# Replicating gate values over partitions through a DRAM scratch instead of 64 shifted copies

## The chip, the cores and the metric

The kernel runs on one core of one Trainium2 chip. The metric is the device time of one execution in microseconds. The profile's span, from the first to the last instruction, is about 1.9 us shorter than that time. Most executions of one kernel lie within a few tenths of a microsecond, so a difference of 0.5 us (0.2%) is about the smallest that five rounds can show. In the views, PE stands for the matmuls of TensorE and PEld for its weight loads, ACT for ScalarE, DVE for VectorE, POOL for GpSimd, SPq for the queue in which SyncE issues DMAs; a PSUM bank is a piece of the memory that matmuls write to.

## The reference

The output is a mix of two branches over 2048 tokens of width 512, with a gate g per token:

```python
g = _sigmoid((x * gate_w).sum(-1, keepdims=True))
a = _A_ref(x, A_wq, A_wk, A_wv, A_wo, A_beta)     # 4 segments of 512 tokens, 32 heads of 16
b = _B_ref(x, B_W_gate, B_W_up, B_W_down)         # gated FFN, 512 -> 1792 -> 512
return g * a + (1 - g) * b
# in _A_ref, per segment s and head:
#   p = softmax(q k^T * scale + causal mask);  a_dot = p v
#   o = sigmoid(beta) * (phi(q) M / (phi(q) z + 1e-6)) + (1 - sigmoid(beta)) * a_dot
#   M, z are then updated with phi(k), v of this segment
```

The change touches only small things: where exp of the gate logit lies in memory, and constants made from beta.

## The kernel before

The kernel builds a list of operations with estimated durations. A list scheduler (`Sched`), whose tie-breaks depend on a seed, then fixes one static order for each engine. So any change of an operation or of the seed can move every instruction. The gate part and the constants:

```python
sc = Sched(seed=59)
...
cst = [act(... V.eb = exp(V.braw) ...)]
cst.append(dve(... V.romgh = V.eb + 1 ...))
cst.append(dve(... V.epsv = V.romgh * EPS ...))
for s2 in range(2):
    for tt in range(4):        # the column of ones, scaled, beside V in vaug
        cst.append(dve(lambda e, s2=s2, tt=tt: e.tensor_copy(V.vaug[:, s2, tt, :, 16], V.romgh[:, :]), 190, ...))
...
for c in range(NSEG):
    # c == 0: POOL multiplies x by gate_w (gml), ACT sums each product (gad); gate_w comes by DMA into gwb
    # c > 0: x is loaded again, DVE multiplies and sums (gate)
    gq["act"].append(act(... gx = exp(V.gl[:, t0:t1]) ..., name="gexp"))
    ...
    for a in range(4):
        for jj in range(4):    # 16 copies a segment, 32 partitions x 4 values each
            dst = V.gexpT[32 * jj:32 * jj + 32, 16 * c + 4 * a:16 * c + 4 * a + 4]
            gq["flex"].append(... dve or act: copy dst <- V.gexp[32 * a:32 * a + 32, t0:t1] ...)
```

The one reader of gexpT is `rdg` on DVE, which scales the attention output of each head group. TensorE runs three kinds of work. Ordinary matmuls use the whole array (projections and FFN, 512 columns). Score quads are four or eight matmuls on 32 rows each (x4 or x8 in the views); each quad writes four PSUM banks that one large exp on ACT (2048 columns) must read before the next quad may write them. PV groups use four column tiles. For the order of the start it matters that ACT has one queue:

```python
acts.append(act(lambda a, e=e: a.activation(V.E[:, e, :, :], PL[:, :, :], ACT.Exp, scale=SCALE), t_act(2048),
                reads=[f"bankL{b}" for b in range(4)], writes=[f"E{e}"], name=f"exp{s}_{tag}"))
```

The softmax here doesn't subtract the row's maximum and nothing guards it: scores larger than these inputs give would overflow.

Of the kernel before, what the change touches and what calls it, by code (L numbers as in the profile page):

```python
# [8 lines left out]
ACT = mybir.ActivationFunctionType  # L9
# [3 lines left out]
F32 = mybir.dt.float32  # L13
# [11 lines left out]
def t_act(n, psum=True, ap=0):  # L25
    return (174.0 if psum else 198.0) + 0.834 * n + 93.0 * ap


def t_dve(n, rate=1):
    return 155.0 + n / rate / 0.96  # L30
# [336 lines left out]
def plan(S, D, F):  # L367
    NT, KT, NF = S // 128, D // 128, F // 128
    return [
        ("xT", [128, KT, S], BF16), ("wq", [128, KT, 512], BF16), ("wk", [128, KT, 512], BF16), ("wv", [128, KT, 512], BF16),  # L370
        ("wo", [128, 4, 512], BF16), ("wg", [128, KT, F], BF16), ("wu", [128, KT, F], BF16), ("wd", [128, NF, 512], BF16),
        ("qT", [128, 8, 512], BF16), ("kT", [128, 4, 512], BF16), ("kp", [128, 12, 512], BF16),
        ("phiq", [128, 4, 512], BF16), ("ek", [128, 4, 512], BF16), ("phik", [128, 4, 512], BF16), ("ttmp", [128, 2, 512], BF16),
        ("vaug", [128, 2, 4, 32, 17], BF16), ("E", [128, 8, 4, 512], BF16),
        ("Tn", [128, 2, 512], F32), ("adT", [128, 512], BF16), ("oTt", [128, 512], BF16),
        ("amem", [128, 2, 512], BF16), ("amemT", [128, 4, 512], BF16), ("oT", [128, 8, 512], BF16),
        ("hT", [128, 20, 512], BF16), ("rl", [128, 3, 512], BF16), ("osb", [128, 3, 512], BF16),
        ("Mbd", [128, 4, 136], F32), ("Mbd16", [128, 4, 136], BF16), ("mumask", [128, 2, 136], BF16), ("mutmp", [128, 2, 136], F32),
        ("braw", [128, 32], BF16), ("eb", [128, 32], F32), ("romgh", [128, 32], F32), ("epsv", [128, 32], F32),
        ("gexp", [128, NT], F32), ("omg", [128, NT], F32), ("gexpT", [128, NT * 4], F32), ("c2g", [128, 2, 4, 32], F32), ("gwb", [128, 512], BF16), ("gl", [128, NT], F32),  # L380
        ("rden", [128, 32], F32), ("rdg", [128, 32], F32), ("rdm", [128, 128], F32), ("pm8", [128, 8], F32), ("pm", [128, 2], F32), ("ident", [128, 128], BF16),
    ]


def build_kernel(nc, A_x, A_wq, A_wk, A_wv, A_wo, A_beta, W_g, W_u, W_d, gate_w, out):
    _, S, D = A_x.shape
    F = W_g.shape[1]
    assert D == 512 and S % 512 == 0 and F % 128 == 0
    NSEG, KT, NF, NT = S // 512, D // 128, F // 128, S // 128
    EPS, SCALE = 1e-6, 16 ** -0.5  # L390
    sc = Sched(seed=59)
    T = {}
    with contextlib.ExitStack() as stack:
        for name, shape, dt in plan(S, D, F):
            T[name] = stack.enter_context(nc.sbuf_tensor(name, shape, dt))
        PL = stack.enter_context(nc.psum_tensor("psL", [128, 4, 512], F32))
        PA = [stack.enter_context(nc.psum_tensor(f"psA{i}", [128, 512], F32)) for i in range(4)]
        for st in sc.streams:
            sc.sem[st] = stack.enter_context(nc.semaphore(f"s_{st}"))
        program(sc, nc, T, PL, PA, A_x, A_wq, A_wk, A_wv, A_wo, A_beta, W_g, W_u, W_d, gate_w, out, NSEG, KT, NF, NT, EPS, SCALE)  # L400
        with nc.Block() as block:
            sc.emit(block)
    return sc


def program(sc, nc, T, PL, PA, A_x, A_wq, A_wk, A_wv, A_wo, A_beta, W_g, W_u, W_d, gate_w, out, NSEG, KT, NF, NT, EPS, SCALE):
    V = type("V", (), T)

    def op(eng, fn, occ, **k):
        return sc.add(Op([(eng, fn, occ)], **k))  # L410
# [7 lines left out]
    def dve(fn, occ, **k):  # L418
        return op("dve", fn, occ, **k)

    def act(fn, occ, **k):
        return op("act", fn, occ, **k)

    def pool(fn, occ, **k):
        return op("pool", fn, occ, **k)

    def dma(eng, fn, nbytes, occ=500.0, **k):
        return op(eng, fn, occ, dma=True, nbytes=nbytes, **k)
# [81 lines left out]
    for i in range(4):  # L510
# [5 lines left out]
        dst = V.xT[:, :, i * 128:(i + 1) * 128]  # L516
# [10 lines left out]
    cst = [act(lambda e: e.activation(V.eb[:], V.braw[:], ACT.Exp), 300, reads=["braw"], writes=["eb"], name="eb")]  # L527
    cst.append(dve(lambda e: e.tensor_scalar(V.romgh[:], V.eb[:], 1.0, None, ALU.add), 190, reads=["eb"], writes=["romgh"], name="romgh"))
    cst.append(dve(lambda e: e.tensor_scalar(V.epsv[:], V.romgh[:], EPS, None, ALU.mult), 190, reads=["romgh"], writes=["epsv"], name="epsv"))
    for s2 in range(2):  # L530
        for tt in range(4):
            cst.append(dve(lambda e, s2=s2, tt=tt: e.tensor_copy(V.vaug[:, s2, tt, :, 16], V.romgh[:, :]), 190, reads=["romgh"], writes=[f"vone{s2}_{tt}"], name="vone"))
    sc.queue(0, [t for t in cst if t.eng == "act"])
    sc.queue(1, [t for t in cst if t.eng == "dve"])

    gexpT_r = {}
    gq = {"pe": [], "act": [], "dve": [], "flex": [], "pool": [], "sp": []}
    for c in range(NSEG):
        t0, t1 = 4 * c, 4 * c + 4
        gx = V.gexp[:, t0:t1]  # L540
        if c == 0:
            for t in range(4):
                gq["pool"].append(pool(lambda e, t=t: e.tensor_tensor(V.Tn[:, t % 2, :], V.hT[:, t, :], V.gwb[:], ALU.mult), 1250, reads=[f"hT{t}", "gwb"], writes=[f"Tn{t % 2}"], name=f"gml{t}"))  # L543
                gq["act"].append(act(lambda e, t=t: e.activation(V.Tn[:, t % 2, :], V.Tn[:, t % 2, :], ACT.Copy, accum_out=V.gl[:, t:t + 1]), t_act(512, False) + 100, reads=[f"Tn{t % 2}"], writes=[f"Tn{t % 2}", f"gl{t}"], name=f"gad{t}"))
        else:
            for t in range(t0, t1):
                ld = dma("sp", lambda e, t=t: e.dma_start(V.osb[:, 2, :], A_x[0, t * 128:(t + 1) * 128, :]), 1 << 17, writes=["osb2_0", "osb2_1"], name=f"ldxr{t}")
                ld.after = GATE_T[c] + 4000.0 * (t - t0)
                gq["sp"].append(ld)
                gq["dve"].append(dve(lambda e, t=t: e.tensor_tensor_reduce(out=V.osb[:, 2, :], in0=V.osb[:, 2, :], in1=V.gwb[:], scale=1.0, scalar=0.0, op0=ALU.mult, op1=ALU.add, accum_out=V.gl[:, t:t + 1]),  # L550
                                     t_dve(512) + 70, reads=["osb2_0", "osb2_1", "gwb"], writes=["osb2_0", "osb2_1", f"gl{t}"], name=f"gate{t}"))
        gq["act"].append(act(lambda e, t0=t0, t1=t1, gx=gx: e.activation(gx, V.gl[:, t0:t1], ACT.Exp), 215, reads=[f"gl{t}" for t in range(t0, t1)], writes=[f"gexp{c}"], name="gexp"))
        om = V.omg[:, t0:t1]
        gq["dve"].append(dve(lambda e, om=om, gx=gx: e.tensor_scalar(om, gx, 1.0, None, ALU.add), 180, reads=[f"gexp{c}"], writes=[f"omg1{c}"], name="omg1"))
        gq["dve"].append(dve(lambda e, om=om: e.reciprocal(om, om), 250, reads=[f"omg1{c}"], writes=[f"omg{c}"], name="omg"))
        gexpT_r[c] = []
        for a in range(4):
            for jj in range(4):
                dst = V.gexpT[32 * jj:32 * jj + 32, 16 * c + 4 * a:16 * c + 4 * a + 4]
                gq["flex"].append(sc.add(Op([("dve", lambda e, a=a, dst=dst, t0=t0, t1=t1: e.tensor_copy(dst, V.gexp[32 * a:32 * a + 32, t0:t1]), 200),  # L560
                                             ("act", lambda e, a=a, dst=dst, t0=t0, t1=t1: e.activation(dst, V.gexp[32 * a:32 * a + 32, t0:t1], ACT.Copy), 215)],
                                            reads=[f"gexp{c}"], writes=[f"gexpT{c}_{a}{jj}"], name="gexpT")))
                gexpT_r[c].append(f"gexpT{c}_{a}{jj}")

    def c2g(s):
        t0 = 4 * s
# [2 lines left out]
    sc.queue(1, gq["act"])  # L569
    sc.queue(1, gq["pool"])  # L570
    sc.queue(1, gq["dve"])
    sc.queue(2, gq["flex"])
    sc.queue(3, gq["sp"])

    def kslot(s, n):
# [53 lines left out]
        return pes, evs, sbs, acts, sps  # L629

    def va(s):
        return [f"va{s % 2}_{tt}" for tt in range(4)] + [f"vone{s % 2}_{tt}" for tt in range(4)]

    def mu(s):
        pes, ds, ps = [], [], []
# [206 lines left out]
    a, b, c_, d, e_ = proj(0)  # L842
    put(pproj=a, dproj=b, dsb=c_, aphi=d, spk=e_)
    slots = None
    for s in range(NSEG):
# [6 lines left out]
        a, b, c_, d, e_ = att(s, between)  # L852
        put(patt=a, exp=b, pool=c_, datt=d, ppv=e_)
        if s < NSEG - 1:
            a, b, c_ = mu(s)
            put(pmu=a, dmu=b, poolmu=c_)
            a, b, c_, d, e_ = proj(s + 1)
            put(pproj=a, dproj=b, dsb=c_, aphi=d, spk=e_)
        a, b, slots = ffn(s)
        put(pffn=a, effn=b)  # L860
    a, b, c_ = outp(NSEG - 1, slots)
# [39 lines left out]
def bass_gated_mix__memory_aug_infini_attn__glu_gated_reglu__prompt_kernel(  # L901
    nc, A_x, A_wq, A_wk, A_wv, A_wo, A_beta, B_x, B_W_gate, B_W_up, B_W_down, gate_w, out
):
    return build_kernel(nc, A_x, A_wq, A_wk, A_wv, A_wo, A_beta, B_W_gate, B_W_up, B_W_down, gate_w, out)
# [28 lines left out]
```

## Time and profile before

273.07 us median of 3 runs (272.86 to 273.07).

| | before |
|---|---|
| span | 271.2 us |
| PE / DVE / ACT / POOL busy | 97 / 76 / 75 / 37% |
| chain that ended last, on PE | 88% |

The page's line of busy times (us, share of the span, instructions) and its shares of the chain, kernel before:

```profile
PE 263.0 (97%) x2108; PEld 115.1 (42%) x2143; DVE 204.8 (76%) x382; ACT 203.7 (75%) x210; POOL 99.5 (37%) x156
...
PE 88%; ACT 2%; DVE 2%; DMA 2%; issue 2%; POOL 2%; ACTq 1%; DVEq 0%; POOLq 0%
```

What the change takes away, from the groups by form of the kernel before (line, engine, operation, tiles, shapes, count | busy us, mean ns | idle before it):

```profile
L561 ACT ACTIVATE gexpT<-gexp 32x4 f32<-32x4 f32 x57 | 11.6, 203 | 1.4
...
L560 DVE COPY gexpT<-gexp 32x4 f32<-32x4 f32 x7 | 2.4, 344 | 0.2
L532 DVE CAST vaug<-romgh 128x32 bf16<-128x32 f32 x8 | 1.9, 349 | 0.0
```

A busy PE is modelled, so the question whether TensorE ever waits is better asked of its weight loads. The timeline of weight loads of the kernel before, at the start (start us, duration us, what, count, [idle before <- releaser]):

```profile
11.98 0.96 PEld L602 LDWEIGHTS psA<-xT,wk 128*128 128x128 bf16 x5
13.94 0.10 PEld L698 LDWEIGHTS psL<-qT,kp 32*128 32x128 bf16 x4 [1.00 <-DVE kp L616]
14.27 2.70 PEld L600 LDWEIGHTS psA<-wv,xT 128*128 128x128 bf16 x14 [0.23 <-issue]
17.80 0.12 PEld L698 LDWEIGHTS psL<-qT,kp 32*128 32x128 bf16 x8 [0.83 <-ACT E L703]
18.13 0.11 PEld L600 LDWEIGHTS psA<-wv,xT 128*128 128x128 bf16 x2 [0.21 <-issue]
```

(kp is the masked copy of the keys that a quad needs, made on DVE.) Ordinary loads follow one another every 0.216 us. Between the last ordinary load and a quad the least that occurs is 0.522 us, a switch of 0.306 us more. Anything longer is a stall. A load takes 0.10 us, so the last of the five wk loads starts at 11.98 + 0.96 - 0.10 = 12.84; the first quad comes at 13.94, that is 1.10 later, a stall of about 0.57 us. For the second quad, the last load ahead starts at 14.27 + 2.70 - 0.10 = 16.87, and 17.80 is 0.93 later, a stall of 0.41. These two, 0.98 us in all, are the only stalls of note in the whole span. The same two are in the view of PE's waits (us in total, times, longest; counted from the modelled end of the matmul before, so a little less):

```profile
PE psL L698 <- DVE kp L616: 0.5, 1, 0.5
PE psL L698 <- ACT E L703: 0.3, 1, 0.3
```

The second comes from ACT's queue. Its timeline, kernel before: the gate exp, four of the copies to be removed, and an exp for the keys stand before the first attention exp (E), which the second quad needs:

```profile
13.78 0.20 ACT L552 ACTIVATE gexp<-gl 128x4 f32<-128x4 f32 x1
14.01 0.89 ACT L561 ACTIVATE gexpT<-gexp 32x4 f32<-32x4 f32 x4
14.93 1.06 ACT L584 ACTIVATE ek<-kT 128x1024 bf16<-128x1024 bf16 x1
15.89 1.86 ACT L703 ACTIVATE E<-psL 128x2048 bf16<-128x2048 f32 x1
```

### The profile page before, as it was taken

What the parts mean: (1) busy time and instruction counts of PE and PEld (TensorE: products, weight loads), DVE (VectorE), ACT (ScalarE), POOL (GpSimd) and SP (SyncE); (2) the same over time, 40 slices, a digit from 0 to 9 for tenths busy, and PEclk for the clock granted to TensorE, in tenths of its full rate; (3) what the DMA queues carried; (4) which work ended last, traced back from release to release, by engine and by line L of the source; (5) the groups of instructions that cost most, each with busy time, mean ns of one, the idle gap of its engine ahead of it and who ended that gap; (6) DMA issues with size and microseconds to landing.
All of it is one profiled execution on the core that took longest, in us unless ns stands there. A gap on an engine that the chain in (4) does not pass through costs nothing.

```text
span 271.2 us, 5268 instructions
## 1 busy us (share of the span) xinstructions
PE 263.0 (97%) x2108; PEld 115.1 (42%) x2143; DVE 204.8 (76%) x382; ACT 203.7 (75%) x210; POOL 99.5 (37%) x156
## 2 busy tenths in 40 slices
PE   8989999999999999999999999999999999999996
PEld 4433343444444444444343444343434444344444
DVE  4689988899889799999888887877773547776300
ACT  3499998898989987899768779887776768682122
POOL 5614343454533253643333532333333242421000
PEclk9999999999999999999999999999999999999999
DMA  6999953102200143210001220000012000000011
GB/s 192 331 365 238 237 96 69 29 7 55 55 25 19 31 89 97 60 39 2 0 2 39 62 78 22 19 2 1 2 39 52 27 19 22 0 0 4 0 39 41
DMA packets 31017, 17.01 MB, mean 63 GB/s; under 512 B 20880, under 2 KB 30992, under 8 KB 30992
## 3 DMA queue, kind: packets, MB, share of 16 engines
q1 hardware_dynamic: 30272, 16.01, 23.3%
q10 hardware_dynamic: 720, 0.66, 1.0%
q8 instruction: 17, 0.28, 0.4%
q14 instruction: 8, 0.07, 0.1%
HBM read 9.84 MB, written 2.10 MB: 44 GB/s over the span
## 4 chain that ended last, share of the span: by engine, by line
PE 88%; ACT 2%; DVE 2%; DMA 2%; issue 2%; POOL 2%; ACTq 1%; DVEq 0%; POOLq 0%
PE psA L780 36%; PE psA L819 17%; PE psL L698 9%; PE psA L602 8%; PE psA L724 7%; PE psA L812 5%; PE psA L600 4%; DMA gwb<-in_gate_w_dram 2%; POOL Tn L543 2%; PE psA L672 1%; PE psA L643 1%; ACT E L703 1%; ACTq L439 1%; DVE osb L828 1%; PE psA L659 0%
## 5 line engine op out<-in xcount | busy, mean ns | idle before, releaser
L703 ACT ACTIVATE E<-psL 128x2048 bf16<-128x2048 f32 x80 | 150.0, 1875 | 31.1 <-PE psL L698 30.6
L706 POOL TENSOR_SCALAR_AFFINE_SELECT E<-E 128x512 bf16<-128x512 bf16 x128 | 85.4, 685 | 139.6 <-ACT E L703 139.5
L780 PE MATMUL psA<-xT,wg 128*128 128x512 bf16 x213 | 58.0, 380 | 1.1 <-issue 0.8
L780 PE MATMUL psA<-xT,wu 128*128 128x512 bf16 x217 | 58.4, 380 | 0.6 <-issue 0.3
L819 PE MATMUL psA<-wd,hT 128*128 128x512 bf16 (+2 forms) x233 | 53.0, 367 | 0.8 <-issue 0.8
L791 DVE TENSOR_TENSOR hT<-psA,rl 128x512 bf16<-128x512 f32 x56 | 38.2, 683 | 13.5 <-PE psA L780 12.5
L698 PE MATMUL psL<-qT,kp 32*128 32x384 bf16 (+3 forms) x512 | 31.7, 301 | 0.8 <-DVE kp L616 0.5
L780 PEld LDWEIGHTS psA<-xT,wu 128*128 128x128 bf16 x224 | 20.4, 98 | 25.8 <-issue 3.2
L819 PEld LDWEIGHTS psA<-wd,hT 128*128 128x128 bf16 x238 | 20.9, 98 | 23.8 <-issue 4.0
L780 PEld LDWEIGHTS psA<-xT,wg 128*128 128x128 bf16 x224 | 20.1, 98 | 24.9 <-issue 3.1
L729 DVE STREAM_TRANSPOSE Tn<-psA 128x512 f32<-128x512 f32 x32 | 20.9, 692 | 7.9 <-PE psA L724 7.9
L789 DVE TENSOR_SCALAR rl<-psA 128x512 bf16<-128x512 f32 x30 | 20.6, 688 | 4.0 <-PE psA L780 3.0
L698 PEld LDWEIGHTS psL<-qT,kp 32*128 32x128 bf16 x512 | 8.9, 92 | 34.0 <-ACT E L703 14.0
L788 ACT ACTIVATE rl<-psA 128x512 bf16<-128x512 f32 x26 | 15.5, 595 | 10.3 <-PE psA L780 10.2
L724 PE MATMUL psA<-E,vaug 128*17 128x256 bf16 (+3 forms) x512 | 20.2, 300 | 0.0
L829 ACT ACTIVATE osb<-psA,omg 128x512 bf16<-128x512 f32 (+2 forms) x10 | 6.4, 645 | 13.7 <-PE psA L812 13.1
L812 PE MATMUL psA<-wo,oT 128*128 128x512 bf16 (+2 forms) x64 | 15.9, 366 | 0.3 <-issue 0.2
L602 PE MATMUL psA<-xT,wk 128*128 128x512 bf16 x62 | 15.9, 380 | 0.2 <-DVE ttmp L585 0.2
L602 PE MATMUL psA<-xT,wq 128*128 128x512 bf16 x61 | 15.5, 380 | 0.5 <-issue 0.3
L600 PE MATMUL psA<-wv,xT 128*128 128x512 bf16 x61 | 14.7, 380 | 0.4 <-issue 0.3
L724 PEld LDWEIGHTS psA<-E,vaug 128*17 128x17 bf16 x512 | 10.7, 90 | 9.4 <-issue 2.5
L609 DVE CAST qT<-psA 128x512 bf16<-128x512 f32 x16 | 10.7, 676 | 3.4 <-PE psA L602 3.3
(71 smaller groups left out, 233.0 us busy)
## 6 DMA issues: line engine op xcount, KB each, us to landing
out_dram<-osb SPq DMA_DIRECT2D x15, 128.0 KB, 1.7
wg<-in_B_W_gate_dram SPq DMA_DIRECT2D x8, 224.0 KB, 5.4
wu<-in_B_W_up_dram SPq DMA_DIRECT2D x8, 224.0 KB, 5.7
wd<-in_B_W_down_dram SPq DMA_DIRECT2D x1, 1792.0 KB, 10.5
osb<-in_A_x_dram SPq DMA_DIRECT2D x12, 128.0 KB, 2.0
wk<-in_A_wk_dram SPq DMA_DIRECT2D x4, 128.0 KB, 5.6
wv<-in_A_wv_dram SPq DMA_DIRECT2D x4, 128.0 KB, 4.9
wo<-in_A_wo_dram SPq DMA_DIRECT2D x1, 512.0 KB, 5.0
```

The lines of the kernel that those rows point to most:

```text
L600: ins = e.matmul(A(ep)[:, :], lhsT=V.xT[:, kt, tok + col * 128:tok + (col + 1) * 128], rhs=w[:, kt, :], start=(kt == 0), stop=(kt == KT - 1))
L602: ins = e.matmul(A(ep)[:, :], lhsT=w[:, kt, col * 128:(col + 1) * 128], rhs=V.xT[:, kt, tok:tok + 512], start=(kt == 0), stop=(kt == KT - 1))
L698: ins = q.matmul(PL[:, jj, o:o + w], lhsT=V.kp[32 * jj:32 * jj + 32, kslot(s, n), 128 * j:128 * j + 128], rhs=V.qT[32 * jj:32 * jj + 32, q ...
L703: acts.append(act(lambda a, e=e: a.activation(V.E[:, e, :, :], PL[:, :, :], ACT.Exp, scale=SCALE), t_act(2048), reads=[f"bankL{b}" for b i ...
L706: pools.append(pool(lambda g, ap=ap: g.affine_select(out=ap, in_=ap, compare_op=ALU.is_ge, fill=0.0, base=0, pattern=[[0, 4], [1, 128]], c ...
L724: ins = q.matmul(A(ep)[32 * jj:32 * jj + 17, c:512], lhsT=V.vaug[:, s % 2, j, 8 * G + 2 * jj + p, :], rhs=V.E[:, e, jj, o:o + w], start=(j ...
L729: ds.append(dve(lambda e, p=p, ep=eps[p]: e.transpose(V.Tn[:, p, :], A(ep)[:, :]), t_dve(512), writes=[f"Tn{p}"], name=f"tr{s}_{G}_{p}", e ...
L780: ins = e.matmul(A(ep)[:, :], lhsT=w[:, kt, f * 128:(f + 1) * 128], rhs=V.xT[:, kt, c * 512:(c + 1) * 512], start=(kt == 0), stop=(kt == K ...
L789: ("dve", lambda e, ep=eg, r=r: e.tensor_scalar(V.rl[:, r, :], A(ep)[:, :], 0.0, None, ALU.max), t_dve(512))],
L791: evs.append(dve(lambda e, ep=eu, r=r, hs=hs: e.tensor_tensor(V.hT[:, hs, :], A(ep)[:, :], V.rl[:, r, :], ALU.mult), t_dve(512), reads=[f" ...
L812: ins = e.matmul(A(ep)[:, 0:c1 - c0], lhsT=V.oT[:, o0 + G, i * 128:(i + 1) * 128], rhs=V.wo[:, G, c0:c1], start=st_ and G == 0, stop=sp_ a ...
L819: ins = e.matmul(A(ep)[:, 0:c1 - c0], lhsT=V.hT[:, slots[f], i * 128:(i + 1) * 128], rhs=V.wd[:, f, c0:c1], start=st_ and f == f0, stop=sp ...
```

## The change

The intent is to free ACT and DVE from 64 small copies: for each segment, the 128x4 gate values are written to a DRAM scratch and read back four times, already in the replicated layout. The eight copies of the ones column become one strided operation, and the constants made from beta are pushed later. The scheduler's seed is chosen anew.

```diff
-    sc = Sched(seed=59)
+    sc = Sched(seed=258)
...
-    for s2 in range(2):
-        for tt in range(4):
-            cst.append(dve(... V.vaug[:, s2, tt, :, 16], V.romgh[:, :] ..., name="vone"))
+    cst.append(dve(... V.vaug[:, :, :, :, 16].rearrange("q s t h -> q (s t) h"), V.romgh[:, :].unsqueeze(1).to_broadcast([128, 8, 32]) ..., name="vone"))
+    cst[0].after = 20000.0
+    cst[2].after = 40000.0
...
+    gscr = nc.dram_tensor("gscr", [NSEG, 4, 32, 4], F32).ap()
...
-        for a in range(4):
-            for jj in range(4):
-                ... the 16 copies ...
+        gq["sp"].append(dma("sp", lambda e, c=c, gx=gx: e.dma_start(gscr[c].rearrange("a r t -> (a r) t"), gx), ..., name=f"gwr{c}"))
+        grd = dma("sp", lambda e, ...: [e.dma_start(gdst[32 * j:32 * j + 32, :].rearrange("r (a t) -> r a t", t=4), gsrc) for j in range(4)], ..., occ=2000.0, name=f"grd{c}")
+        grd.nd = 4
+        gq["sp"].append(grd)
```

More of the change, by code (lines that the diff above doesn't have):

```diff
@@ L529, in program @@
     cst.append(dve(lambda e: e.tensor_scalar(V.epsv[:], V.romgh[:], EPS, None, ALU.mult), 190, reads=["romgh"], writes=["epsv"], name="epsv"))
-    for s2 in range(2):
-        for tt in range(4):
-            cst.append(dve(lambda e, s2=s2, tt=tt: e.tensor_copy(V.vaug[:, s2, tt, :, 16], V.romgh[:, :]), 190, reads=["romgh"], writes=[f"vone{s2}_{tt}"], name="vone"))
+    cst.append(dve(lambda e: e.tensor_copy(V.vaug[:, :, :, :, 16].rearrange("q s t h -> q (s t) h"), V.romgh[:, :].unsqueeze(1).to_broadcast([128, 8, 32])), 420, reads=["romgh"], writes=["vone"], name="vone"))
+    cst[0].after = 20000.0
+    cst[2].after = 40000.0
     sc.queue(0, [t for t in cst if t.eng == "act"])
@@ L536, in program @@
     gexpT_r = {}
-    gq = {"pe": [], "act": [], "dve": [], "flex": [], "pool": [], "sp": []}
+    gscr = nc.dram_tensor("gscr", [NSEG, 4, 32, 4], F32).ap()
+    gq = {"pe": [], "act": [], "dve": [], "pool": [], "sp": []}
     for c in range(NSEG):
@@ L555, in program @@
         gq["dve"].append(dve(lambda e, om=om: e.reciprocal(om, om), 250, reads=[f"omg1{c}"], writes=[f"omg{c}"], name="omg"))
-        gexpT_r[c] = []
-        for a in range(4):
-            for jj in range(4):
-                dst = V.gexpT[32 * jj:32 * jj + 32, 16 * c + 4 * a:16 * c + 4 * a + 4]
-                gq["flex"].append(sc.add(Op([("dve", lambda e, a=a, dst=dst, t0=t0, t1=t1: e.tensor_copy(dst, V.gexp[32 * a:32 * a + 32, t0:t1]), 200),
-                                             ("act", lambda e, a=a, dst=dst, t0=t0, t1=t1: e.activation(dst, V.gexp[32 * a:32 * a + 32, t0:t1], ACT.Copy), 215)],
-                                            reads=[f"gexp{c}"], writes=[f"gexpT{c}_{a}{jj}"], name="gexpT")))
-                gexpT_r[c].append(f"gexpT{c}_{a}{jj}")
+        gexpT_r[c] = [f"gexpT{c}"]
+        gq["sp"].append(dma("sp", lambda e, c=c, gx=gx: e.dma_start(gscr[c].rearrange("a r t -> (a r) t"), gx), 2048, reads=[f"gexp{c}"], writes=[f"gscr{c}"], name=f"gwr{c}"))
+        gdst, gsrc = V.gexpT[:, 16 * c:16 * c + 16], gscr[c].rearrange("a r t -> r a t")
+        grd = dma("sp", lambda e, gdst=gdst, gsrc=gsrc: [e.dma_start(gdst[32 * j:32 * j + 32, :].rearrange("r (a t) -> r a t", t=4), gsrc) for j in range(4)], 8192, occ=2000.0, reads=[f"gscr{c}"], writes=[f"gexpT{c}"], name=f"grd{c}")
+        grd.nd = 4
+        gq["sp"].append(grd)
     def c2g(s):
@@ L571, in program @@
     sc.queue(1, gq["dve"])
-    sc.queue(2, gq["flex"])
     sc.queue(3, gq["sp"])
@@ L631, in va @@
     def va(s):
-        return [f"va{s % 2}_{tt}" for tt in range(4)] + [f"vone{s % 2}_{tt}" for tt in range(4)]
+        return [f"va{s % 2}_{tt}" for tt in range(4)] + ["vone"]
     def mu(s):
```

## The prediction

> **What bounds the kernel now.** TensorE. The page gives PE 97% busy (263.0 of 271.2 us), DVE 76%, ACT 75%; the chain that ended last is 88% PE. Busy PE is modelled, so I checked the timeline of weight loads: ordinary 512-column matmuls start every 0.216 us nearly everywhere. The exceptions are structural: entering a 32-row attention-score quad costs 0.522 instead of 0.216 us, leaving it about 0.317. The Trainium skill ("TensorEngine Tiling (Array Packing)", Key Properties) says that changing tiling mode drains TensorE; this trace agrees, with about 0.3 us a switch. Spacing stretched by a wait I find at two places only: before the first score quad at 12.8 us (0.57 us, DVE kp) and before the second at 16.9 us (0.41 us, ACT exp), together 0.98 us. After 20 us DVE, ACT and DMA cause no stall worth naming. Startup before the first projection is 6.35 us, the tail after the last weight load 2.6 us.
>
> **Removed.** 64 gexpT copies: 57 on ACT at 203 ns (11.6 us), 7 on DVE at 344 ns (2.4 us), from the groups by form. Eight ones-column copies (1.9 us busy on DVE) become one, 128x256 strided, estimated 0.5 us. In all 11.6 us of ACT and 3.5 to 4 us of DVE.
>
> **Added.** Four times a 2 KB write to DRAM and four small reads back: 20 issues on SyncE. Estimate from this trace: issue 0.3 to 0.6 us each, landing about 2 us as for the x rows (median 2.0), so about 6 us from gate exp to gexpT. For the first segment the write queues behind the 1.8 MB wd load, and the reads behind phik and xT transposes at 1.3 us each; I expect gexpT near 40 us and its first reader near 44.
>
> **Moved.** All engines' orders change with the scheduler's seed. PE has the same 2143 matmuls and the same 80 score-quad and 16 PV visits; one direct quad-to-PV transition fewer, about 0.3 us more switching. Replaying the after order with the trace's spacings gives 261.6 us against 261.3, without stalls. At the start, DVE no longer idles 0.96 us for romgh (behind eb on ACT) ahead of the first kT copy, nor runs epsv (0.59) before the kp masks. The first quad stands four matmuls earlier and should start near 12.5 us without a wait. ACT no longer puts four gexpT copies and an ek exp before the first attention exp: it starts near 14.0 instead of 15.9 us. But PE reaches the second quad near 15.3 and must wait for that exp until about 15.95: a stall of about 0.65. Startup stalls fall from 0.98 to 0.65.
>
> **Critical path.** Nearly nothing of the 15 us removed lies on it. Net: -0.3 us startup, +0.3 us switching, and a little for an order presumably picked for time. I predict 272.9 us, 272.1 to 274.2 us in 8 of 10. Faster by over 2%: 0.01; within 2%: 0.97; slower: 0.02.
>
> **What would show it.** Right: PE still about 97%, ACT busy near 192 us, DVE near 201 us; first attention exp at 14 us; only the second quad stalls early; rdg never waits for DMA. Wrong: rdg waiting for a gexpT read; quads or ordinary matmuls waiting on DVE or ACT after 20 us; SyncE held by the landing write, delaying xT, phik or amemT transposes.
>
> **What would make it wrong.** The new static order may meet real durations badly (a PSUM bank freed late, DVE blocked at romgh behind eb near 22 us), each up to 1 us; scratch reads of 16-byte runs landing far later than 2 us.

## The result, and the profile after

The changed kernel takes 273.01 us (median of 6 runs, 272.55 to 273.39), the kernel before 273.01 us (272.66 to 273.20). The ratio is 1.0003, with a 95% interval of 0.999 to 1.0015: the same. (A ratio is the mean time of one kernel's fast runs over that of the other's fast runs of the same rounds, so not quite the ratio of the medians.)

The page's busy line and chain, kernel after:

```profile
PE 262.8 (97%) x2108; PEld 114.4 (42%) x2143; DVE 200.8 (74%) x366; ACT 193.5 (71%) x155; POOL 99.6 (37%) x156
...
PE 92%; DMA 2%; POOL 2%; issue 1%; ACT 1%; ACTq 1%; DVE 0%; POOLq 0%
```

ACT has 10.2 us less to do and DVE 4.0 us less; PE has the same. The work is gone and the time is not. Weight loads at the start, kernel after:

```profile
9.16 2.47 PEld L600 LDWEIGHTS psA<-xT,wk 128*128 128x128 bf16 x12
12.06 0.10 PEld L696 LDWEIGHTS psL<-qT,kp 32*128 32x128 bf16 x4 [0.42 <-DVE kp L614]
12.38 0.55 PEld L600 LDWEIGHTS psA<-xT,wk 128*128 128x128 bf16 x4 [0.23 <-issue]
13.05 1.18 PEld L598 LDWEIGHTS psA<-wv,xT 128*128 128x128 bf16 x6
15.82 0.12 PEld L696 LDWEIGHTS psL<-qT,kp 32*128 32x128 bf16 x8 [1.59 <-ACT E L701]
```

The first quad now follows without a stall. But the second comes 15.82 - (13.05 + 1.18 - 0.10) = 1.69 us after the last ordinary load, a stall of 1.17 us. It is the only one of note left, and PE's waits name it:

```profile
PE psL L696 <- ACT E L701: 1.1, 1, 1.1
```

ACT's timeline, kernel after. The copies and ek no longer stand in front, so the first attention exp starts 2 us earlier than before; but it cannot start before the gate exp, which ends a chain of the gate_w load, POOL's products and ACT's sums:

```profile
13.04 0.63 ACT L545 ACTIVATE Tn<-Tn 128x512 f32<-128x512 f32 x1 [0.44 <-POOL Tn L544]
...
13.80 0.20 ACT L553 ACTIVATE gexp<-gl 128x4 f32<-128x4 f32 x1
13.91 1.86 ACT L701 ACTIVATE E<-psL 128x2048 bf16<-128x2048 f32 x1
```

In the order of before, TensorE has 46 ordinary projection matmuls to do ahead of the second quad; in the new order 38. So it arrives there earlier and waits longer. The span of each profiled run splits as follows (startup: to the first projection's weight load; stalls: spacing beyond 0.216 and 0.522 us; tail: from the last weight load; the rest is the difference):

| us | startup | stalls | tail | rest | span |
|---|---|---|---|---|---|
| before | 6.35 | 0.98 | 2.64 | 261.2 | 271.18 |
| after | 5.89 | 1.17 | 2.63 | 261.3 | 271.02 |

The DRAM trip itself is hidden. SyncE's timeline, kernel after, first segment:

```profile
21.16 0.51 SPq L439 DMA_DIRECT2D wd<-in_B_W_down_dram  x1
21.78 2.99 SPq L558 DMA_DIRECT2D gscr<-gexp  x1
25.47 6.11 SPq L620 DMA_TRANSPOSE phik<-ek  x4
31.63 1.26 SPq L458 DMA_TRANSPOSE xT<-in_A_x_dram  x1
32.98 1.95 SPq L560 DMA_DIRECT2D gexpT<-gscr  x4
```

The reader rdg, in the view of the tile gexpT, kernel after (duration min/median/max in ns, then first and last start in us):

```profile
L735 DVE TENSOR_TENSOR rdg<-rden,gexpT x16: 198/306/764, 48.6 to 246.9; 128x32 f32<-128x32 f32 x16
```

The reads were issued by 34.9 us. In the trace the last of these four landed at 36.4 us (median of all 16: 2.2 us from issue to landing); the first reader runs at 48.6 us and never waits for them.

### The profile page after: what moved, and what is told of

Same layout as the page of the kernel before. It is cut to its first block, busy times and chain, and to the rows that moved or that the text cites. A ratio compares the mean times of both kernels' runs of the same rounds, so it can differ in the third digit from the quotient of the medians.

```text
span 271.0 us, 5223 instructions
## 1 busy us (share of the span) xinstructions
PE 262.8 (97%) x2108; PEld 114.4 (42%) x2143; DVE 200.8 (74%) x366; ACT 193.5 (71%) x155; POOL 99.6 (37%) x156
## 4 chain that ended last, share of the span: by engine, by line
PE 92%; DMA 2%; POOL 2%; issue 1%; ACT 1%; ACTq 1%; DVE 0%; POOLq 0%
PE psA L778 37%; PE psA L817 18%; PE psL L696 9%; PE psA L600 8%; PE psA L722 7%; PE psA L810 5%; PE psA L598 5%; DMA gwb<-in_gate_w_dram 2%; POOL Tn L544 2%; PE psA L641 1%; PE psA L670 1%; ACTq L439 1%; ACT E L701 1%; PE psA L657 0%; ACT Tn L545 0%
## 5 line engine op out<-in xcount | busy, mean ns | idle before, releaser
L704 POOL TENSOR_SCALAR_AFFINE_SELECT E<-E 128x512 bf16<-128x512 bf16 x128 | 84.5, 678 | 136.3 <-ACT E L701 136.2
L778 PE MATMUL psA<-xT,wg 128*128 128x512 bf16 x214 | 58.9, 380 | 0.7 <-issue 0.3
L778 PE MATMUL psA<-xT,wu 128*128 128x512 bf16 x215 | 56.5, 380 | 0.9 <-issue 0.6
L786 ACT ACTIVATE rl<-psA 128x512 bf16<-128x512 f32 x28 | 16.7, 598 | 15.6 <-PE psA L778 13.1
L787 DVE TENSOR_SCALAR rl<-psA 128x512 bf16<-128x512 f32 x28 | 19.2, 687 | 4.6 <-PE psA L778 3.8
L827 ACT ACTIVATE osb<-psA,omg 128x512 bf16<-128x512 f32 (+2 forms) x11 | 7.1, 648 | 14.0 <-PE psA L810 13.1
L600 PE MATMUL psA<-xT,wq 128*128 128x512 bf16 x63 | 16.3, 380 | 0.3 <-DVE mutmp L644 0.2
```

Of the source, the lines that this page charges most:

```text
L600: ins = e.matmul(A(ep)[:, :], lhsT=w[:, kt, col * 128:(col + 1) * 128], rhs=V.xT[:, kt, tok:tok + 512], start=(kt == 0), stop=(kt == KT - 1))
L704: pools.append(pool(lambda g, ap=ap: g.affine_select(out=ap, in_=ap, compare_op=ALU.is_ge, fill=0.0, base=0, pattern=[[0, 4], [1, 128]], c ...
L778: ins = e.matmul(A(ep)[:, :], lhsT=w[:, kt, f * 128:(f + 1) * 128], rhs=V.xT[:, kt, c * 512:(c + 1) * 512], start=(kt == 0), stop=(kt == K ...
L787: ("dve", lambda e, ep=eg, r=r: e.tensor_scalar(V.rl[:, r, :], A(ep)[:, :], 0.0, None, ALU.max), t_dve(512))],
```

## The experiments

An ordinary edit would let the scheduler shuffle everything, so most experiments keep an order. Such a kernel runs the scheduler on one program (before, seed 59, or after, seed 258), records each operation's engine, place and PSUM bank, and builds another program in that order, with the listed operations inserted or moved (operation, engine, operation it follows). With no edits, the built programs were the same as the originals, instruction for instruction and wait for wait. All experiments computed the right result.

The theory: the kernel is bound by TensorE's fixed work, and only the first two quads' stalls can be won. The rivals: ACT and DVE time counts and was given back by the trip or the order; or the trip costs.

### Does ACT time count, does PE time count?

act_dose puts 75 small copies back on ACT, one after each later attention exp; pe_dose puts 28 more ordinary matmuls into the second segment. Both keep the order of the changed kernel.

```diff
+ act: V.dose[0:32, :] <- V.gexp[0:32, 0:4]          # act_dose: after each exp from the second head group on
+ if c == 1 and kt == 0: e.matmul(<same group, start=True, stop=True>)   # pe_dose: before each gate and up group
```

> The changed kernel in its own order, with 75 copies of 32x4 put back on ACT, one after each attention exp from the second head group on (203 ns each in the trace before, 15 us in all; their results are not used). Theory (TensorE-bound, ACT idle time before each exp takes them up): same as the changed kernel within 0.3 us, ACT busy about 208 us. Rival (ACT time counts): several us slower, up to 15.

> The changed kernel in its own order, with 28 more ordinary 512-column matmuls, one ahead of each gate and up group of the second token segment (overwritten at once, result unchanged). Theory (TensorE-bound): 28 x 0.216 = 6.0 us slower, 279.0 (5.5 to 6.5 more). Rival (TensorE's 97% is modelled and hides slack): clearly less than 4 us.

act_dose: 272.94 us against 272.78 for before, ratio 1.0004 (0.9991 to 1.0016), as the changed kernel. pe_dose: 279.24 us, ratio 1.024 (1.0224 to 1.0256), about 6.5 us more for an expected 6.0. The added copies in the groups by form of act_dose:

```profile
L758 ACT ACTIVATE dose<-gexp 32x4 f32<-32x4 f32 x75 | 14.1, 188 | 0.0
```

The page's busy line of act_dose, to be held against that of the changed kernel:

```profile
PE 266.4 (98%) x2143; PEld 114.5 (42%) x2143; DVE 201.4 (74%) x366; ACT 199.2 (73%) x230; POOL 99.8 (37%) x156
```

My figure for ACT's busy time was wrong: 14.1 us of copies raise it by only 5.7 us (to 199.2, not 208), because each copy starts before the exp ahead of it has ended. So this dose put back about half of the busy time that the change took from ACT (10.2 us), and none of it at the start, where ACT does hold up a quad. Within that the verdict stands: 75 added ACT instructions, more than the 57 removed, cost nothing, while TensorE work is paid in full. In the profiled run of pe_dose all of it can be found: without startup, stalls and tail its span leaves 267.4 us, 6.05 more than the changed kernel's 261.3, and 28 x 0.216 is 6.05. The 6.5 is between medians of timed runs, and against the kernel before.

The two runs also repeat the changed kernel's start, for they add nothing before 30 us. Their second quads, first act_dose, then pe_dose:

```profile
16.18 0.12 PEld L751 LDWEIGHTS psL<-qT,kp 32*128 32x128 bf16 x8 [1.60 <-ACT E L756]
...
15.41 0.12 PEld L751 LDWEIGHTS psL<-qT,kp 32*128 32x128 bf16 x8 [0.44 <-ACT E L756]
```

The gate_w load landed at 8.68 us in act_dose, 8.32 in the changed kernel's trace and 7.96 in pe_dose; the first attention exp started at 14.27, 13.91 and 13.50, and the second quad at 16.18, 15.82 and 15.41, 1.91 us after the exp each time. So the gate_w load sets the second quad's start in this order. The stalls themselves differ from run to run: 0.45 and 1.18 us at the two quads in act_dose, none and 1.17 in the changed kernel's trace, 0.27 and 0.01 in pe_dose.

### Does the order matter?

Here the scheduler was left free: the changed code with the old seed, and the old code with the new seed.

```diff
-    sc = Sched(seed=258)
+    sc = Sched(seed=59)      # new_seed59, from the changed kernel
-    sc = Sched(seed=59)
+    sc = Sched(seed=258)     # old_seed258, from the kernel before
```

> The changed kernel with the scheduler's old seed 59: the code change without a new choice of order. The order that comes out has runs of 40 and 34 ordinary matmuls without a score quad and three quads back to back. Theory (the order decides): slower than both, 274 to 282 us, with waits of quads for ACT's attention exps. Rival (the change fixes the time, the seed does not matter): 273.0 within 0.3 us.

> The kernel before with the new seed 258. Replay of its order with the spacings of the trace before gives 262.0 us of stall-free TensorE time against 261.3 (fewer direct quad-to-PV transitions). Theory (the order decides): 273.5 to 275 us. Rival (seed does not matter): 273.0 within 0.3 us.

old_seed258: 273.34 us, ratio 1.0023 (1.001 to 1.0037), slower than before by about 0.6 us; a little less than I expected. Its trace does not bear out the reason I gave, the switching: without startup (5.82 us), stalls and tail its span leaves about 261.0 us, no more than before's 261.2. What grew is the stalls, about 2.2 us against 1.0, most of them at the first three quads. new_seed59: 286.22 us, ratio 1.0487 (1.0451 to 1.0523), worse than I expected. Its longest PE wait:

```profile
PE psL L696 <- ACT E L701: 8.5, 6, 2.3
```

Its busy times by stretch (stretch and its length in us; busy us of PE, PEld, DVE, ACT and POOL; granted clock, DMA share, GB/s):

```profile
85.00:90.00 5.00, 1.01 (x12) 0.23 (x12) 4.76 (x9) 4.28 (x4) 2.54 (x4) 0.66 0.35 84
90.00:95.00 5.00, 4.16 (x20) 1.24 (x20) 1.53 (x4) 3.63 (x3) 2.14 (x3) 0.50 0.26 52
```

Quads stand back to back near 85 us, each waits for an attention exp, TensorE is busy 1.0 us in 5, and its clock falls to one half: its ordinary loads came 0.43 us apart near 92 us, twice 0.216. The Trainium skill ("TensorE: Matmul & The Clock Gate", Part 1) states that the array falls to half its clock after about 3.4 us of idleness; this trace agrees on the half, but not on the 3.4 us: the granted clock was 1.00 from 85 to 86 us, 0.82 from 86 to 87 and 0.50 after that, so it fell near 86.6 us (estimated from the 0.82), when TensorE had idled 1.40 us, worked 0.40 and idled 0.7. So the seed is part of the change: the same code with the old seed is 13 us slower. What the new seed buys is only to be back where the old code was.

### One part at a time, in the order of before

route_old changes only the replication, const_old only the constants, both_old both.

```diff
  BASE = before, seed 59
+ route_old EDITS: gwr0 sp after ldwd, grd0 sp after kT20_1; gwr1..3 sp after gexp, grd1..3 after gwr
+ const_old EDITS: eb act after exp0_0B0, romgh dve after hm0_0, epsv dve after hm0_2; one vone
+ both_old  EDITS: both lists
```

> The order of all engines of the kernel before is kept; only the gate replication goes through DRAM (64 copies out, 20 DMA issues in). Theory (TensorE-bound; only the two early stalls can be won): the 4 gexpT copies no longer stand before the first attention exp, so it starts 0.9 us earlier and the second quad's stall (0.41 us) goes; the first quad's stall (0.57 us) stays. Expect 0.3 to 0.5 us less than before (about 272.6), ACT busy about 192 us. Rival (ACT and DVE time counts all along, and the new order of the changed kernel gave the gain back): 2 us or more faster. Second rival (the DRAM trip costs): slower by over 0.5 us, with rdg or SyncE waiting.

> The order of the kernel before is kept; only eb, romgh and epsv come later and the 8 ones copies are one. Theory: the first quad's stall (0.57 us) goes, as DVE no longer idles for romgh before the first kT copy; but the second quad still waits for the first attention exp, which gexpT copies and ek hold to 15.9 us on ACT, so its stall grows from 0.41 to about 0.98 us: time unchanged, within 0.2 us of before. Rival (each removed stall is won by itself): 0.57 us faster.

> The whole change, but in the order of the kernel before. Theory: both early stalls go (0.98 us) but for 0.1 us at the second quad: 0.7 to 0.9 us faster than before, about 272.2, that is also about 0.8 us faster than the changed kernel with its own order. Rival (the change is worth nothing whatever the order): same as before within 0.2 us.

const_old: 272.93 us, as before's 272.93, ratio 1.0 (0.9984 to 1.0016). It is the clearest of the three. Weight loads, const_old:

```profile
13.30 0.10 PEld L751 LDWEIGHTS psL<-qT,kp 32*128 32x128 bf16 x4 [0.42 <-DVE kp L669]
13.63 2.70 PEld L653 LDWEIGHTS psA<-wv,xT 128*128 128x128 bf16 x14 [0.23 <-issue]
17.85 0.12 PEld L751 LDWEIGHTS psL<-qT,kp 32*128 32x128 bf16 x8 [1.52 <-ACT E L756]
```

The first quad no longer stalls, and the second starts at 17.85 against 17.80 us before: the stall has moved there whole (1.10 us against 0.57 and 0.41). The second quad waits for ACT's first attention exp whatever the first quad does, so removing the first stall alone wins nothing.

route_old: 272.57 us median, ratio 0.9995 (0.9973 to 1.0017), with one run at 274.18 us and a granted clock of 0.994. The direction fits, the interval does not decide. Its profile shows what was expected of the mechanism: the second quad has no stall, the first still waits for DVE. That wait was longer in this run (0.90 us against 0.57), so the second quad, at 17.58 us, came only 0.22 us earlier than before.

both_old: its profiled run took 271.84 us (span 270.1, no stall at either quad), but all six ran from 271.84 to 274.16, median 273.01, ratio 1.0002 (0.9979 to 1.0026). By the numbers the expectation failed. As the first reader stood at 37.8 us there, less than 2 us after the reads should land, I suspected the DRAM trip. (In the trace of the profiled run the last read had landed at 35.15 us, 2.6 us ahead of its reader, so that run at least gave no ground for it.)

### The trip's place, in the order of before

both_early issues the first segment's trip ahead of wo and wd. both_tight and trip_late place its reads two and five transposes after phik instead of none.

```diff
+ both_early EDITS: gwr0 sp after ldx1_1, grd0 sp after ldx1_3; the rest as both_old
+ both_tight EDITS: gwr0 sp after ldwd,   grd0 sp after ldx2_1; the rest as both_old
+ trip_late  EDITS: ldx3_0 sp after ldx2_3, gwr0 sp after ldwd, grd0 sp after ldx3_0; the rest as both_old
```

> The whole change in the order of the kernel before, as in both_old, but the first segment's DRAM trip is issued between the second token segment's transposes, ahead of wo and wd. In the profile of both_old the reads were issued only at 32.2 us, after the write landed behind wd, and the first reader rdg ran at 37.8 us, about 1.5 us after they landed. Theory (the timed runs of both_old, 271.8 to 274.2 us, are slow where the trip came too late for rdg): gexpT lands near 25 us, 12 us before rdg, and the runs lie close together near 272.2, 0.6 to 0.9 us faster than before. Rival (the spread is that of the startup loads and of the clock, the trip has no part in it): median and spread as in both_old, 273.0, over 1.5 us wide.

> As both_old, but the first segment's reads from DRAM are issued two transposes later, near 34.7 us, to land near 39 us, about 1.2 us after DVE wants them for the first rdg. Theory (the trip is the weak place of this order): the profile shows DVE waiting 1 to 2 us at rdg for a DMA and TensorE losing up to 1 us near 40 us; 0.5 to 1.2 us slower than both_early. Rival (DVE has that much slack there): DVE waits, TensorE does not, and the time is as both_early within 0.2 us.

> As both_tight, whose trip was not late after all: its reads were issued at 32.9 us, because SyncE waits for the write (behind wd) until about 32 us anyway. Here the reads come three transposes later, to be issued near 36.6 to 38.6 us and to land near 40.8 us, about 2.7 us after DVE reaches the first rdg (38.1 us in both_tight). Theory (the trip is hidden only while it lands before its reader; DVE then holds up the PSUM banks): DVE waits 2.5 to 3 us for the DMA at rdg, TensorE stalls 1 to 2 us near 41 us, and the time is 1 to 2 us above the 272.1 us of both_tight. Rival (DVE slack takes up even that): TensorE does not stall and the time stays near 272.1.

both_early: 272.02 us (271.82 to 272.72) against 273.01, ratio 0.9962 (0.995 to 0.9973), 1 us faster than before. both_tight: 272.13 us (271.83 to 272.27), ratio 0.9961, so my expectation for it failed: its reads were not late. SyncE waits for the write, which sits behind wd, until about 32 us in any case, so moving the reads behind two transposes only filled that wait (issue at 32.85 instead of 32.16 us), and rdg did not wait. both_tight is in effect both_old once more, on another chip, and there the whole change in the old order is 1 us faster (both_early, both_tight and early_gate below, which show this, ran on one chip). Weight loads of both_early:

```profile
13.28 0.10 PEld L751 LDWEIGHTS psL<-qT,kp 32*128 32x128 bf16 x4 [0.42 <-DVE kp L669]
13.61 2.70 PEld L653 LDWEIGHTS psA<-wv,xT 128*128 128x128 bf16 x14 [0.23 <-issue]
16.73 0.12 PEld L751 LDWEIGHTS psL<-qT,kp 32*128 32x128 bf16 x8 [0.42 <-ACT E L756]
```

Neither quad stalls; the second starts 1.07 us earlier than before (16.73 against 17.80), which is the whole gain of this profiled run: the two stalls (0.98) and an earlier first projection (6.16 us against 6.35), less a short wait at 6.5 us (0.11).

trip_late does make the reads late: 273.06 us, ratio 1.0018 (0.9995 to 1.0041), with runs from 272.57 to 274.84. DVE's timeline, trip_late:

```profile
40.58 0.21 DVE L790 TENSOR_TENSOR rdg<-rden,gexpT 128x32 f32<-128x32 f32 x1 [2.46 <-DMA gexpT<-gscr]
40.71 0.69 DVE L842 TENSOR_SCALAR rl<-psA 128x512 bf16<-128x512 f32 x1
```

PE's waits, trip_late:

```profile
PE psA L833 <- DVE rl L842: 0.4, 1, 0.4
```

DVE stands 2.46 us at rdg, the eviction behind it (rl) comes late, and TensorE loses about 1.0 us between 40.7 and 45.6 us (0.41, 0.43 and 0.18 in its load spacing). So the trip can cost, where it comes late. Whether that made both_old spread on its chip is not shown: const_old and gate_late ran narrow (0.9 us) on that chip, route_old and both_old (last read landed 3.4 and 2.6 us ahead of its reader in their traces) ran wide (2.2 and 2.3 us, route_old's slowest run at the lower clock), but both_tight, with 0.2 us to spare (37.88 against 38.07), ran narrow on another chip. The rival, the spread of the chip and of the startup loads, is as likely: the kernel before ran 1.4 us wide on the chip of both_old and 0.8 on that of both_tight. That stays open.

### The gate chain out of the way

gate_late keeps the changed kernel's order and puts the last gate sum and the gate exp behind the first attention exp; early_gate does the same to both_early.

```diff
+ gate_late  EDITS: gad3, gexp act after exp0_0A0; kexp0_1 after exp0_0B0; kexp0_3, eb after exp0_0A1; romgh dve after kphi0_3
+ early_gate EDITS: gad3, gexp act after exp0_0A0; kexp0_1 after exp0_0A1; kexp0_3 after exp0_0B1; the rest as both_early
```

> The changed kernel in its own order, but on ACT the last gate sum and the gate exp come after the first attention exp, and ek and eb after later ones. Theory: the second quad's stall in the changed kernel (1.17 us in its trace) is the chain gate_w load, POOL products, ACT sums, gate exp, first attention exp; the first attention exp now starts near 12.7 instead of 13.9 us and the stall falls below 0.2 us: 0.9 to 1.2 us faster than the changed kernel, about 272.0. Rival (that stall is only where a later, equal wait shows first): the wait moves to the third or a later quad and the time stays at 273.0.

> both_early and, as in gate_late, the last gate sum and the gate exp behind the first attention exp, the two ek exps behind the fourth and fifth. Theory: no stall is left at the first two quads whatever the gate_w load does; span about 270.1, time 272.0, 0.8 to 1.1 us faster than before. Rival: the moved ek exps or gate sums delay later attention exps, and quads three to six wait: no faster than both_early.

gate_late: 272.37 us against 272.93, ratio 0.9977 (0.9961 to 0.9992): faster than before by 0.6 us, where the changed kernel was the same (in other rounds); less than the 0.9 to 1.2 us I expected. The second quad in the timeline of weight loads, gate_late (the six loads ahead of it start at 13.63):

```profile
13.63 1.18 PEld L653 LDWEIGHTS psA<-wv,xT 128*128 128x128 bf16 x6
15.23 0.12 PEld L751 LDWEIGHTS psL<-qT,kp 32*128 32x128 bf16 x8 [0.42 <-ACT E L756]
```

The first attention exp in ACT's timeline, gate_late:

```profile
13.09 1.88 ACT L756 ACTIVATE E<-psL 128x2048 bf16<-128x2048 f32 x1 [0.39 <-PE psL L751]
```

No stall is left at the second quad, nor does one show up later. Of the 1.17 us of the changed kernel's trace about half is won: this run started its first projection at 6.35 us, 0.46 later than the trace after did, and lost another 0.35 there. early_gate: 272.03 us, ratio 0.9961 (0.9949 to 0.9973), no faster than both_early. That order has no stall left to take, so the move is not worth anything in it.

## Why the prediction was right

The time was right: 272.9 us predicted, 273.01 measured, within 2% as forecast.

- "TensorE" bounds the kernel: shown by the two doses, and by the kept orders. 75 small copies on ACT, 5.7 us of busy time, changed nothing; 28 matmuls cost 6.5 us. And with ACT and DVE relieved in the order of before, the profiled run of both_early still has 261.2 us outside startup, stalls and tail, as the kernel before.
- "Nearly nothing of the 15 us removed lies on it": shown. ACT fell by 10.2 us and DVE by 4.0 us, as said (193.5 us for a predicted 192, 200.8 for 201), and the time stayed.
- The first quad "without a wait", and the first attention exp "near 14.0": the exp started at 13.91 us, and the first quad had no stall in that trace (0.45 and 0.27 us in the two repeats of this start, act_dose and pe_dose).
- "A stall of about 0.65" at the second quad: the place and the cause were right, the size was not; it was 1.17 us. The quad starts when the gate chain lets it, at 15.82 us for a predicted 15.95. But in that run TensorE began its projections at 5.89 us instead of 6.35, and what it gained in the startup loads it spent waiting for the same exp. That is why the sum came out right: startup and stalls together fell from 7.33 to 7.06 us, 0.27 for a predicted 0.3. So close a match is luck: in act_dose and pe_dose, with the same start, the sum was 7.6 and 6.7 us (waits of 0.2 us among the first projections included). And the earlier start is not shown to be the change's doing: with the start of this order it came at 5.81, 5.89 and 6.17 us, and in gate_late at 6.35.
- "About 0.3 us more switching": in the split above the rest grew by about 0.1 us, from 261.2 to 261.3. The term was over-sized, and is too small for the runs to show.
- The trip: reads issued at 33 to 35 us and the last landed at 36.4, for a predicted 40; first reader at 48.6 for a predicted 44. It never waited, as predicted; the slack was larger than I thought.
- What I had not seen: the change was worth something. In the order of before, with the trip early, it gives 1 us (0.38%), in the main both stalls. In its own order the freed ACT time was turned into an earlier arrival at the same gate chain, with eight matmuls fewer to fill the time.

## What to carry to other kernels

Before costing the work that a change removes, list the few waits of the engine that binds and ask which of them the change shortens. Here 15 us of work had 1 us of waits behind it. Of the two stalls here, in series, removing the first alone won nothing and removing both won 1 us. A small value that is needed late (here the gate exp, first read at 21 us, and its replicated copy at 48.6 us) should not stand in an in-order queue ahead of the operation that the binding engine waits for. Where a scheduler fixes the order, test a change in a kept order before judging it: the seed alone was worth from 0.6 to 13 us.

## What the Trainium skill lacked or had wrong

- "TensorE: Matmul & The Clock Gate", Back-to-back issue gap: this section gives about 131 ns a matmul as the sustained spacing for 512 columns with a weight load each, and calls 216 ns the isolated gap. Here the sustained spacing is 216 ns, all through the span; 28 added matmuls cost 6.05 us in the profiled run (0.216 us each) and about 6.5 us between the timed medians.
- "TensorEngine Tiling (Array Packing)", Key Properties: it says that a change of mode drains TensorE, but not what that costs. Here 0.306 us going in (0.522 instead of 0.216 us) at 77 of the 80 quads of the kernel before; at the other three the matmul ahead was short (128 or 136 columns) and the quad's load came 0.21 us after its own.
- "Perfetto Trace Analysis", Identifying the Most-Contended Engine: it takes the busy share of weight loads, beside the share of peak FLOPs, as a measure of how near TensorE is to its limit. Here that share was 42% in a kernel with 1 us of stalls; a 98 ns load per 216 ns matmul cannot exceed 45%. The spacing of the loads was the better measure.
- "DMA: Bandwidth & Descriptors", Anatomy of one DMA: its fixed 2.0 us are for another issue path. Here, issued by SyncE, a 2 KB write landed after 1.4 us (median of four) and the 2 KB reads after 2.2 us, but the first write, behind the 1.8 MB load of wd, took 9.4 us. I saw no figure for such a wait on the page.
